# Two-bank PSUM evacuations, LayerNorm's root on another engine and a look-ahead scheduler in a fused attention and feed-forward block

## The chip, the cores and the metric

The kernel runs on one core of a Trainium2 chip. The metric is the time of one execution in microseconds (us), lower is better. A run is one execution; medians and ranges below are over the runs of one kernel. PE is the matmul engine, DVE the vector engine, ACT the scalar engine, POOL the third elementwise engine, and SP the engine that issues most DMA.

"Same" means within 2%.

## The reference

One block with S = 2048 rows, D = 1024, F = 3584 and H = 32 heads of 32:

```python
def _A_ref(x, wqkv, wo):                       # linear attention
    q, k, v = ...                              # x @ wqkv, split into heads
    phi = lambda t: jnp.where(t > 0, t + 1, jnp.exp(t)) + 1e-06
    pq, pk = (phi(q), phi(k))
    kv = jnp.einsum('bhsd,bhse->bhde', pk, v)
    z = jnp.einsum('bhsd->bhd', pk)
    num = jnp.einsum('bhqd,bhde->bhqe', pq, kv)
    den = jnp.einsum('bhqd,bhd->bhq', pq, z)[..., None] + 1e-06
    return (num / den)... @ wo

def _B_ref(x, w_gate, w_up, w_down):
    return _gelu(x @ w_gate) * (x @ w_up) @ w_down

mod = (_silu(c) @ w_mod).reshape(c.shape[0], 6, 1, -1)   # sa, ca, ga, sb, cb, gb
h = _layernorm(x) * (1 + ca) + sa
x = x + ga * _A_ref(h, A_wqkv, A_wo)
h = _layernorm(x) * (1 + cb) + sb
x = x + gb * _B_ref(h, B_w_gate, B_w_up, B_w_down)
```

## The kernel before

The program has eight phases, named here by what PE does: start (modulation, first LayerNorm, the first V rows), K/V/Q projections, merge (the last Q products, the KV matrix, the second modulation set), projection (the denominators and the output projection, then LayerNorm 2), gate/up for half the rows, down, gate/up and down for the other half. The K/V/Q and merge phases use a scheme of seven products where plain blocking needs eight; its elementwise additions run on ACT and DVE, straight from PSUM.

PSUM, the memory that PE writes its results to, is eight banks, cut into small rings. Evacuating a bank means reading a result out of it, so that PE can use the bank again. Each call hands out the next bank of a ring:

```python
class Banks:
    def __call__(self, dt=FP32):
        self.i += 1
        b = psm[:, self.lo + (self.i - 1) % self.n, :]
        return b if dt == FP32 else b.bitcast(dt)
...
QA, QB = Banks(0, 1), Banks(2, 3)
psX = Banks(4, 7)
psC, psB = Banks(0, 3), Banks(4, 7)
```

One bank holds one matmul result of 128x512 float32 (the Trainium skill, "PSUM — Partial Sum Buffer", says the same in its table of terms: one matmul output is at most one bank), so no evacuation in the kernel before has more than 512 columns. In the projection phase, sixteen tiles of 128 rows need two banks each, and two denominators are computed ahead of each tile:

```python
def den_start(b, g):
    psd = psX()
    te.matmul(psd, lhsT=Dbd[:, g, :], rhs=pqT[b][:, g, :], start=True, stop=True)
    lnd = lnd_ring()
    ac.activation(out=lnd, in_=psd, func=AF.Ln, bias=eps6, scale=1.0)      # L876
    rden = rden_ring()
    ac.activation(out=rden, in_=lnd, func=AF.Exp, scale=-1.0)
    return lambda: tt_op(pqT[b][:, g, :], pqT[b][:, g, :], rden, ALU.mult)

def wo_tile(tt, banks):
    ...
    for half in range(NHD):
        cs = slice(half * NW, (half + 1) * NW)
        psw = banks()
        for g in range(KD):
            te.matmul(psw, ...)                                            # L1029
        tt_op(xt[:, cs], psw, xt[:, cs], ALU.add)                          # L480
    gp.dma_start(out=x2_scr[b][tl * P:(tl + 1) * P, :], in_=xt)
    return xt

# projection phase
for tt in range(NTT):
    for _ in range(min(2, len(den_todo))):
        den_start(*den_todo.pop(0))()
    xt = wo_tile(tt, psX if tt < 4 else psC)
    ...
    if tt < 2 * TT:
        ln2_xhat(tt, xt, *ln2_stats(xt, act_rstd))   # LayerNorm 2: two bn_stats, bn_aggr, root, scale
```

`tt_op` is one line for every two-operand DVE operation. In traces it is L480 before the change and L495 after it; experiments that add lines move it to L488 and so on.

The code records operations, and a list scheduler (`Plan`) orders them before they are issued. PE keeps the recorded order. Every other engine is reordered by priority, in forward and backward sweeps over a cost model of the operations, and the order of the best modelled sweep is used.

## Time and profile before

| | before |
|---|---|
| median of the first 3 runs | 772.71 us (772.5 to 773.33) |
| profiled span | 770.3 us |
| PE busy | 752.5 us, 98% |
| DVE busy | 555.1 us, 72% |

The page's table of busy time in the kernel before has one entry for each engine (share of the span, number of instructions); the other line is the summary of the chain of work that ended last, by engine.

```profile
PE 752.5 (98%) x3672; PEld 345.1 (45%) x3697; DVE 555.1 (72%) x1104; ACT 378.1 (49%) x664; POOL 74.4 (10%) x159
PE 82%; DVE 6%; ACT 4%; DMA 4%; issue 1%; POOL 1%; SPq 1%; DVEq 0%; POOLq 0%; ACTq 0%
```

PE is the bound, and all that the other engines do matters only where PE waits for them. The chain is 82% PE and has 10% of DVE and ACT in it, so there are such places. The windows view of the kernel before finds them. Its columns are start:end and length of the stretch, then the busy time of PE, PEld, DVE, ACT and POOL with instruction counts, then the granted clock, the DMA share and GB/s.

```profile
core 0: us, PE busy (x) PEld busy (x) DVE busy (x) ACT busy (x) POOL busy (x), PEclk, DMA share, GB/s
31.60:98.00 66.40, 65.22 (x354) 31.35 (x362) 52.44 (x128) 41.95 (x70) 17.76 (x34) 1.00 0.46 144
170.00:198.00 28.00, 27.64 (x154) 12.01 (x154) 26.90 (x60) 26.51 (x50) 0.00 (x0) 1.00 0.11 35
198.00:225.00 27.00, 24.54 (x110) 10.64 (x110) 25.93 (x59) 19.14 (x41) 6.48 (x12) 1.00 0.60 188
225.00:256.00 31.00, 31.00 (x145) 14.06 (x144) 24.52 (x48) 22.19 (x38) 5.93 (x11) 1.00 0.91 266
```

From 198 to 225 us PE is idle for 27.00 - 24.54 = 2.46 us, while DVE is busy for 25.93 of 27.00 us. The view of waits on PE, for 30 to 440 us of the kernel before, names what ended each idle time (engine, line, what it waited for: total us, times, longest).

```profile
PE psum L874 <- ACT mem L876: 2.2, 2, 1.2
PE psum L1123 <- ACT mem L721: 0.7, 2, 0.5
PE psum L863 <- DVE mem L480: 0.6, 1, 0.6
PE psum L897 <- ACT mem L517: 0.5, 1, 0.5
PE psum L1029 <- DVE mem L480: 0.2, 1, 0.2
```

L874 is the denominator matmul; it waits for the logarithm on ACT (L876) to free its bank. L1123 is in gate/up, L863 in the K/V phase, L897 in the merge. The timeline of PE in the kernel before shows the two long waits (start, duration, operation, in brackets the idle time before it and its releaser):

```profile
205.90 3.66 PE L1029 MATMUL psum<-mem 128*128 128x512 f16 x16
210.51 0.38 PE L874 MATMUL psum<-mem 128*128 128x512 bf16 x1 [0.96 <-ACT mem L876]
212.13 0.38 PE L874 MATMUL psum<-mem 128*128 128x512 bf16 x1 [1.24 <-ACT mem L876]
```

Why is ACT late? Its own timeline in the kernel before answers:

```profile
208.69 0.29 ACT L570 ACTIVATE mem<-mem 128x1 f32<-128x1 f32 x1 [3.58 <-DVE mem L559]
209.77 0.69 ACT L876 ACTIVATE mem<-psum,mem 128x512 f32<-128x512 f32 x1
```

ACT was not busy. Its next instruction in the queue was LayerNorm 2's root (L570), which waited 3.58 us for DVE to aggregate statistics (L559), and the logarithm that PE needed stood behind it. ACT issues its queue in order, as the Trainium skill, "TensorE: Matmul & The Clock Gate", section "Architectural detail: the array is 16× 32×32, not 1× 128×128", says of ACT and DVE; the 3.58 us agree. The groups of the kernel before by form, 168 to 230 us, show what fills DVE (operation, count, busy us, mean ns, idle before):

```profile
L480 DVE TENSOR_TENSOR mem<-psum,mem 128x512 bf16<-128x512 f32 x16 | 11.0, 685 | 0.1
L480 DVE TENSOR_TENSOR mem<-mem 128x512 bf16<-128x512 bf16 x24 | 9.2, 410 | 0.0
L888 DVE SCALAR_TENSOR_TENSOR mem<-psum,mem 128x512 f16<-128x512 f32 x16 | 10.4, 684 | 0.1
```

By these durations a projection tile that also has LayerNorm costs DVE about 2 x 0.69 (additions) + 2 x 0.69 (statistics) + 0.21 + 0.54 + 2 x 0.41 (denominators) = 4.3 us, and PE 18 matmuls of 0.215 us = 3.9 us.

### The profile page before, as it was taken

What the parts mean: (1) busy time and instruction counts of PE and PEld (TensorE: products, weight loads), DVE (VectorE), ACT (ScalarE), POOL (GpSimd) and SP (SyncE); (2) the same over time, 40 slices, a digit from 0 to 9 for tenths busy, and PEclk for the clock granted to TensorE, in tenths of its full rate; (3) what the DMA queues carried; (4) which work ended last, traced back from release to release, by engine and by line L of the source; (5) the groups of instructions that cost most, each with busy time, mean ns of one, the idle gap of its engine ahead of it and who ended that gap; (6) DMA issues with size and microseconds to landing.
All of it is one profiled execution on the core that took longest, in us unless ns stands there. A gap on an engine that the chain in (4) does not pass through costs nothing.

```text
span 770.3 us, 10215 instructions
## 1 busy us (share of the span) xinstructions
PE 752.5 (98%) x3672; PEld 345.1 (45%) x3697; DVE 555.1 (72%) x1104; ACT 378.1 (49%) x664; POOL 74.4 (10%) x159
## 2 busy tenths in 40 slices
PE   6999999999999999999999999999999999999998
PEld 2454445444344444444444444444444444444444
DVE  7878785489997878799887553686777777646254
ACT  3665666569778577775454203215445444430000
POOL 1431300000121122211010000010000000000000
PEclk9999999999999999999999999999999999999999
DMA  9847120780289666766757558852341323355441
GB/s 303 304 131 239 50 69 0 267 321 14 97 243 259 208 209 211 236 196 200 214 181 261 175 195 239 234 156 79 85 110 55 109 72 93 130 184 206 167 153 49
DMA packets 132259, 129.12 MB, mean 168 GB/s; under 512 B 32752, under 2 KB 111216, under 8 KB 131184
## 3 DMA queue, kind: packets, MB, share of 16 engines
q1 hardware_dynamic: 123680, 105.40, 44.2%
q0 software_dynamic: 6176, 20.98, 7.4%
q10 hardware_dynamic: 2352, 2.10, 0.8%
q8 instruction: 29, 0.48, 0.3%
q14 instruction: 22, 0.18, 0.1%
HBM read 98.04 MB, written 23.07 MB: 157 GB/s over the span
## 4 chain that ended last, share of the span: by engine, by line
PE 82%; DVE 6%; ACT 4%; DMA 4%; issue 1%; POOL 1%; SPq 1%; DVEq 0%; POOLq 0%; ACTq 0%
PE psum L1123 41%; PE psum L1228 22%; PE psum L852 5%; PE psum L1029 5%; PE psum L818 4%; PE psum L790 3%; DVE mem L480 3%; DMA mem<-in_A_wqkv_dram 3%; DVE mem L557 1%; DMA mem<-in_B_w_down_dram 1%; ACT mem L709 1%; PE psum L863 1%; ACT mem L721 1%; ACT mem L711 1%; DVE mem L888 1%
## 5 line engine op out<-in xcount | busy, mean ns | idle before, releaser
L1123 PE MATMUL psum<-mem 128*128 128x512 f16 x1568 | 339.1, 379 | 0.7 <-ACT mem L721 0.7
L480 DVE TENSOR_TENSOR mem<-psum,mem 128x512 f16<-128x512 f32 (+4 forms) x296 | 197.9, 680 | 106.8 <-ACT mem L721 39.5
L480 DVE TENSOR_TENSOR mem<-mem 128x1024 f16<-128x1024 bf16 (+9 forms) x415 | 213.8, 539 | 36.5 <-DMA mem<-in_B_w_down_dram 5.4
L1123 PEld LDWEIGHTS <-mem 128*128 128x128 f16 (+1 forms) x1568 | 153.5, 98 | 186.0 <-issue 1.3
L721 ACT ACTIVATE mem<-psum 128x512 f32<-128x512 f32 x226 | 132.2, 594 | 161.9 <-PE psum L1123 81.6
L1228 PE MATMUL psum<-mem 128*128 128x512 f16 (+2 forms) x789 | 169.1, 375 | 0.5
L1228 PEld LDWEIGHTS <-mem 128*128 128x128 f16 x798 | 78.1, 98 | 91.4
L1136 ACT ACTIVATE mem<-mem 128x512 f16<-128x512 f16 x84 | 52.8, 629 | 78.8 <-DVE mem L480 78.7
L852 PE MATMUL psum<-mem 128*128 128x512 bf16 x244 | 57.4, 379 | 1.0 <-DMA mem<-in_A_wqkv_dram 0.2
L1029 PE MATMUL psum<-mem 128*128 128x512 f16 x256 | 57.8, 379 | 0.2 <-DVE mem L480 0.2
L818 PE MATMUL psum<-mem 128*128 128x512 f16 x224 | 51.2, 379 | 0.0
L1029 PEld LDWEIGHTS <-mem 128*128 128x128 bf16 x256 | 24.9, 98 | 32.6 <-DVE mem L480 3.0
L790 PE MATMUL psum<-mem 128*128 128x512 f16 (+1 forms) x168 | 38.4, 379 | 0.1
L852 PEld LDWEIGHTS <-mem 128*128 128x128 f16 x256 | 24.8, 98 | 30.3 <-issue 0.7
L709 ACT ACTIVATE mem<-psum 128x512 f16<-128x512 f32 x40 | 23.6, 593 | 21.4 <-PE psum L852 21.3
L818 PEld LDWEIGHTS <-mem 128*128 128x128 f16 (+1 forms) x224 | 21.4, 98 | 26.6 <-issue 2.1
L557 DVE BATCH_NORM_STATS2 mem<-mem 128x6 f32<-128x512 bf16 x48 | 31.2, 681 | 1.6 <-DMA mem<-in_A_x_dram 1.2
L1008 ACT ACTIVATE mem<-mem 128x512 f16<-128x512 f16 x28 | 20.3, 799 | 18.7 <-DMA mem<-xhs 18.7
L714 DVE TENSOR_SCALAR mem<-mem 128x512 f16<-128x512 f16 x56 | 16.1, 289 | 18.3 <-ACT mem L709 17.9
L790 PEld LDWEIGHTS <-mem 128*128 128x128 f16 x168 | 16.2, 98 | 18.6 <-issue 0.3
L1251 DVE TENSOR_TENSOR mem<-psum,mem 128x512 f16<-128x512 f32 x16 | 11.0, 690 | 17.8 <-PE psum L1228 17.8
L711 ACT ACTIVATE mem<-psum 128x512 f16<-128x512 f32 x40 | 23.7, 595 | 0.0
(115 smaller groups left out, 426.8 us busy)
## 6 DMA issues: line engine op xcount, KB each, us to landing
mem<-in_B_w_gate_dram SPq DMA_DIRECT2D x28, 512.0 KB, 4.1
mem<-in_B_w_up_dram SPq DMA_DIRECT2D x28, 512.0 KB, 5.8
mem<-ts SPq DMA_DIRECT2D x8, 1792.0 KB, 7.0
mem<-in_w_mod_dram SPq DMA_DIRECT2D x24, 512.0 KB, 6.1
mem<-in_B_w_down_dram SPq DMA_DIRECT2D x6, 1792.0 KB, 8.4
mem<-in_A_x_dram SPq DMA_DIRECT2D x32, 256.0 KB, 3.9
mem<-in_B_w_down_dram SPq DMA_DIRECT2D x14, 512.0 KB, 6.3
ts<-mem POOLq DMA_DIRECT2D x14, 512.0 KB, 3.6
```

The costliest lines, as they stand in the source:

```text
L480: ve.tensor_tensor(out=out, in0=a, in1=b, op=op)
L557: ve.bn_stats(out=stats[:, cb, :], in_=xt[:, cb * BW:(cb + 1) * BW])
L709: ac.activation(out=e, in_=t, func=AF.Exp)
L711: ac.activation(out=r, in_=t, func=AF.Relu)
L721: ac.activation(out=t, in_=ps, func=AF.Copy)
L790: te.matmul(ps, lhsT=A[:, k, i * P:(i + 1) * P], rhs=B[:, k, :], start=(start and k == 0), stop=(k == KH - 1), skip_group_check=True)
L818: te.matmul(o, lhsT=W[:, k, (j0 + i) * P:(j0 + i + 1) * P], rhs=h_form(a, k), start=(start and k == 0), stop=(k == KH - 1), skip_group_che ...
L852: te.matmul(ps, lhsT=hr1[b][:, k, tl * P:(tl + 1) * P], rhs=Wk[:, k, n * NW:(n + 1) * NW], start=(k == 0), stop=(k == KD - 1))
L1029: te.matmul(psw, lhsT=pqT[b][:, g, tl * P:(tl + 1) * P], rhs=Wp[:, g, cs], start=(g == 0), stop=(g == KD - 1))
L1123: te.matmul(ps, lhsT=a[:, u, k, :], rhs=b[:, k, :], start=(start and k == 0), stop=(k == KH - 1), skip_group_check=True)
L1136: ac.activation(out=t, in_=src, func=AF.Gelu_apprx_tanh)
L1228: te.matmul(ps, lhsT=a[:, i, q * P:(q + 1) * P], rhs=b[:, i, :], start=(start and i == 0), stop=(i == NPR - 1), skip_group_check=True)
```

## The change

The intent is fewer and larger evacuations. Two neighbouring banks become one tile of 128x1024, and one instruction reads both. The diff, cut to its core:

```diff
+        def pair(self):
+            self.i += self.i % 2
+            self.i += 2
+            lo = self.lo + (self.i - 2) % self.n
+            return psm[:, lo:lo + 2, :]
...
-    qf_ring = Ring(176, [TG], FP32, 6)
+    qf_ring = Ring(176, [2, TG], FP32, 3)
...                                          # LayerNorm 1 of the later blocks
-            rstd = pool_rstd(mv)
+            rstd = act_rstd(mv)
...                                          # V and Q products: copies, additions, phi on pairs
-            for i in range(2):
-                ps = QB()
-                mm(ps, i, "a12", "b21", True)
-                comb(ps, st["p1"][i], i, 0, 0)
+            comb(products(QB.pair(), "a12", "b21", True), st["p1"], 0, 0)
...                                          # Q, block (0, 0)
-                ve.scalar_tensor_tensor(out=dst(i, row, col), in0=..., scalar=0.0, in1=...,
-                                               op0=ALU.max, op1=ALU.add)
+                ve.tensor_scalar_max(out=t, in0=t, scalar1=0.0)      # then a plain addition in phi
...
-    def den_start(b, g):
-        psd = psX()
-        te.matmul(psd, lhsT=Dbd[:, g, :], rhs=pqT[b][:, g, :], start=True, stop=True)
+    def den_pair(b, g):
+        psd = psX.pair()
+        for i in range(2):
+            te.matmul(psd[:, i, :], lhsT=Dbd[:, g + i, :], rhs=pqT[b][:, g + i, :], start=True, stop=True)
...                                          # merge: the KV matrix at one stage, its transposes at the next
-                kv_matrix(1)
-                kv_matrix(0)
+                kv_diagonal()
+            if i == 5:
+                kv_transposes()
...
-            cs = slice(half * NW, (half + 1) * NW)
-            psw = banks()
...
-            tt_op(xt[:, cs], psw, xt[:, cs], ALU.add)
+        tt_op(xt, psw.rearrange("p h n -> p (h n)"), xt, ALU.add)
...
-            for _ in range(min(2, len(den_todo))):
-                den_start(*den_todo.pop(0))()
-            xt = wo_tile(tt, psX if tt < 4 else psC)
+            if den_todo:
+                den_pair(*den_todo.pop(0))
+            xt = wo_tile(tt, psX if tt == 0 else psC)
...                                          # the scheduler, five more sweeps with look-ahead
+                    if look and e != "SP":
+                        soon = [o for o in avail[e] if st < o.ready < st + op.cost and o.due < min(op.due, st + op.cost)]
+                        ...                  # hold the engine for a more urgent operation
-        for _ in range(self.ROUNDS):
-            forward()
+        for i in range(2 * self.ROUNDS):
+            forward(i >= self.ROUNDS)
```

The paired Wp scaling in the merge, the order of one modulation step there, the place of one K product among the Q products of each later block, and the places of some buffers also change.

## The prediction

> What bounds it now. The page's busy table has PE at 752.5 us of a 770.3 us span (98%), clock 1.00 in all slices. All its idle time is 17.8 us, which is a ceiling. The windows view places it: 7.6 us before 15.7 us (first loads and LayerNorm), 0.65 us from 15.7 to 31.6, 1.2 us from 31.6 to 98, 0.3 us to 156, 0.6 us to 170, 0.4 us from 170 to 198, 2.5 us from 198 to 225, nothing to 265, about 1.2 us in the whole rest until 760, and 3.6 us at the end. The built program keeps the same matmuls on PE, with a few neighbours exchanged. The change can win only what PE waits in the phases that it edits (31.6 to 225 us): about 5 us, 0.65%.
>
> What it changes. (1) Two-bank evacuations: pairs of 128x512 operations on DVE and ACT become one of 128x1024. From the groups by form, DVE from PSUM takes 685 ns for 512 columns and 550 ns for 387, so 1.08 ns per column: estimated 1.24 us for 1024 against 1.37 us, 0.13 us saved. All-16-bit DVE additions take 418 ns for 512 and 676 ns for 1024, 0.16 us saved. ACT takes 594 ns for 512; the Trainium skill, "ScalarE: Activation LUTs", section "What ACT_TABLE_LOAD costs", gives 186 ns + 0.833 ns per column for immediates, which agrees (613): estimated 1.04 us, 0.15 us saved. (2) The fused max-and-add of Q (692 ns, twice) becomes a max and a plain addition on 1024, about 0.45 us saved, four times. (3) LayerNorm 1 takes its power on ACT (0.29 + 0.20 us) in place of two POOL instructions (about 1.5 us). (4) The output projection leaves the denominators' PSUM banks after its first tile. (5) The scheduler may hold an engine for a more urgent operation.
>
> What lies on the critical path. From 170 to 225 us DVE is 96% busy (52.8 of 55 us) and the chain of waits runs through DVE and ACT, yet PE is idle only 2.9 us: 2.2 us of it is the denominator matmul waiting for the ACT logarithm to free its bank (two waits, about 211 us), 0.2 us a projection bank waiting for DVE. DVE loses about 69 instructions, some 6 us in that window; the projection's share falls to about 4.0 us of DVE per tile, against 3.84 us of PE. I expect (1) and (4) together to remove about 2.3 us of these, and (3) with the shorter DVE queue about 0.7 us (the 0.6 us wait at 85.6 us and small ones). Against that, a pair is freed later than its first half was: refilled after 1.73 us of other matmuls it leaves ACT or DVE some 0.5 us of slack; I allow 0.3 us of new stalls. The feed-forward part should not move.
>
> Sum: 772.7 - 2.3 - 0.7 + 0.3 = 770.0 us, 80% range 767.8 to 772.6. Faster by over 2% 0.01, within 2% 0.97, slower by over 2% 0.02.
>
> Right if: PE busy stays 752 to 753 us; the two denominator waits near 211 us are gone; DVE's busy total falls by 6 to 12 us, ACT's by about 5; POOL's falls. Wrong if: a PSUM hand-over in the Q/V products or merge stalls PE (waits of PE on ACT copies or DVE additions over 2 us in total); the first K weights land much later than 31.5 us because LayerNorm's writes start earlier; or the new scheduling order reaches the feed-forward part.

## The result

| | before | after |
|---|---|---|
| median | 772.87 us (772.08 to 773.68, 14 runs) | 766.64 us (765.78 to 770.34, 11 runs) |
| ratio of the times | | 0.9927 (0.9916 to 0.9939) |
| profiled span | 770.3 us | 766.2 us; a second trace 764.7 us |

A ratio here and below is of the two kernels' fast runs of the same rounds, with a 95% interval; it is not the ratio of the medians quoted, and can differ from it a little. The change saves 6.2 us or 0.8%. That is "same" at the 2% mark, but it is 1.2 us below the predicted range, and more than twice the gain predicted.

The page of the kernel after, first trace, busy times and the summary of the chain:

```profile
PE 751.1 (98%) x3668; PEld 345.8 (45%) x3697; DVE 547.4 (71%) x1015; ACT 375.3 (49%) x611; POOL 61.8 (8%) x132
PE 93%; DMA 4%; DVE 1%; SPq 1%; issue 0%; ACT 0%; DVEq 0%; ACTq 0%
```

The chain is 93% PE now, and DVE and ACT have almost left it. PE's busy time is no guide here: it fell by 1.4 us only, while the time fell by 6. I read the place of the gain from the start times of matmuls instead. Each row is the time from the first matmul of a phase to the first of the next, from the traces; the two traces of the kernel after are the same program.

```
                    start  K/V/Q   merge  projection  gate/up 1  rest
before              29.45  124.78  37.68  63.78       170.23     same
after, first        30.15  123.80  37.41  61.28       169.21     same
after, second       29.94  123.80  37.41  60.01       169.21     same
second - before     +0.49  -0.98   -0.27  -3.77       -1.02      0.0   sum -5.55 (spans: -5.6)
```

Two denominator matmuls (2 x 0.215 = 0.43 us) moved from the projection to the merge. Free of that, the projection lost 3.34 us of stalls and the merge 0.70 us.

The windows of the kernel after, second trace, same stretches and columns as before (the later stretches now begin some microsecond further into the work):

```profile
31.60:98.00 66.40, 65.92 (x361) 31.84 (x366) 56.19 (x132) 45.12 (x81) 8.99 (x17) 1.00 0.46 145
170.00:198.00 28.00, 27.28 (x150) 12.11 (x152) 24.79 (x35) 25.67 (x27) 0.00 (x0) 1.00 0.12 46
198.00:225.00 27.00, 26.89 (x124) 12.22 (x125) 26.04 (x44) 19.64 (x30) 7.02 (x13) 1.00 0.61 178
225.00:256.00 31.00, 30.95 (x144) 14.10 (x144) 23.73 (x34) 18.16 (x27) 5.42 (x10) 1.00 1.09 304
```

From 198 to 225 us PE has 0.11 us of idle time left. DVE is just as busy as it was by its records (26.04 us), with 44 instructions in place of 59. The waits on PE, 30 to 440 us, in the second trace of the kernel after:

```profile
PE psum L886 <- DVE mem L887: 0.3, 1, 0.3
PE psum L846 <- issue: 0.2, 1, 0.2
```

All five lines shown for the kernel before are gone. The first line here is in the merge (L886 is a Wp matmul); the kernel before has 0.2 us at that product, on a line that the excerpt above leaves out. The timeline of PE at the same place, second trace of the kernel after:

```profile
208.41 0.59 PE L873 MATMUL psum<-mem 128*128 128x512 bf16 x2
208.84 3.62 PE L1026 MATMUL psum<-mem 128*128 128x512 f16 x16
212.29 0.59 PE L873 MATMUL psum<-mem 128*128 128x512 bf16 x2
```

No brackets: two denominator matmuls, sixteen of the projection, two denominators, without a gap. The groups of the kernel after, second trace, 168 to 230 us, answer the question what a pair costs:

```profile
L495 DVE TENSOR_TENSOR mem<-psum,mem 128x1024 bf16<-128x1024 f32 x9 | 11.0, 1218 | 0.0
L495 DVE TENSOR_TENSOR mem<-mem 128x1024 bf16<-128x1024 bf16 x14 | 9.3, 668 | 0.0
L887 DVE SCALAR_TENSOR_TENSOR mem<-psum,mem 128x1024 f16<-128x1024 f32 x8 | 9.7, 1218 | 0.9 <-PE psum L886 0.9
```

By its record, a pair from PSUM takes 1218 ns against 2 x 685 = 1370 ns, and from SBUF, the other on-chip memory (`mem` in the views), 668 ns against 2 x 410 = 820 ns: 0.15 us less each, as predicted (1.24 us and 676 ns). ACT's plain copies from PSUM take 1018 ns against 2 x 594, near the 1039 ns that 186 ns + 0.833 ns per column of the page quoted in the prediction give.

What the pair saves the engine is less. Back to back, the next DVE operation starts 84 ns before the record of the one before it ends. From start to start, in the traces of before and after, an addition of 512 columns from PSUM takes 601 ns and one of 16-bit data 335 ns; the pairs take 1134 and 599 ns (medians of those that follow each other without a gap). So a pair saves about 70 ns in either case, half of what the records show. The Trainium skill, "Perfetto Trace Analysis", section "Optimizing Scalar/DVE Operations", gives about 60 ns of overhead for a DVE operation on SBUF and about 125 ns on PSUM, and adds that the profiled latency is about twice this. This agrees that the record exaggerates (0.15 us by the records, 0.07 us by start times), and for SBUF roughly in size; for PSUM the saving is near half the figure.

By start times, a projection tile costs DVE 2 x 0.60 + 2 x 0.60 + 0.12 + 0.45 + 2 x 0.335 = 3.6 us before and 1.13 + 1.21 + 0.12 + 0.45 + 0.60 = 3.5 us after, against PE's 3.9 us. DVE is the faster one in both. Its lateness is brought along from the merge, and it has a deadline, which the next paragraphs find.

### Which matmul waits

A wait line names a source line, not the tile. Counting the projection's matmuls in the traces gives the place of every stall there (length by start times):

```
before            1.12 and 1.40 us   the two denominators just ahead of tile 4
                  0.37 us            tile 4, sixth matmul of its first half
after, first      1.28 us            tile 14, first matmul
after, second     none
```

Tile 4 is the first tile of the second block of 512 rows. Its eight products take the rows divided by their denominators, g = 0 to 7, and the last of these went into the queues just ahead of tile 3, only 3.9 us earlier. Each has to pass a PE matmul, two ACT operations and one DVE multiplication. So this is the deadline: when PE reaches tile 4, DVE and ACT must have caught up, though they come late out of the merge, where DVE is busy for 26.90 of 28 us. After tile 4 the kernel before stalls no more until the end of the phase, which agrees with a DVE that needs 3.6 us per tile.

The change helps here in two ways: its pairs shorten DVE's and ACT's work ahead of tile 4 (35 DVE instructions against 60 from 170 to 198 us), and it puts five pairs of denominators into the merge where there were eight single ones, so that each denominator is one tile earlier. The experiments take these apart as far as they could.

### Where a wait of PE hides

The view of waits shows 2.2 + 0.2 us of PE waiting in the projection phase before the change; the phase has 3.34 us more of stalls than in the second trace after it. The difference is a property of the records. Matmuls of 512 columns start every 0.215 us, and each record lasts 379 ns, with an end that is modelled. So the first 0.16 us of every stall are covered by the record of the matmul before it, and shorter stalls don't show at all. By start times, the two waits of 0.96 and 1.24 us are 1.12 and 1.40 us, the one of 0.21 us is 0.37 us, and three gaps of 0.12 to 0.15 us appear in no view. (A lone pitch of twice 0.215 us at a full clock is left out of these counts: some matmul records are missing from the traces, as 3672 of PE against 3697 weight loads suggest.) The Trainium skill, "Perfetto Trace Analysis", section "Identifying the Most-Contended Engine", warns that matmul busy time is a poor measure because pipelined matmuls look smaller in the trace. Here their records look longer than their pitch, and the consequence is the same: start times, not busy times, show what PE lost.

### The state of the first trace

The first trace after the change is 1.5 us longer than the second: 1.27 us in the projection and 0.21 us in the start. Two lines of its waits on PE, 20 to 440 us, are in these phases:

```profile
PE psum L1026 <- DVE mem L495: 1.1, 1, 1.1
PE psum L566 <- DMA mem<-in_w_mod_dram: 0.6, 1, 0.6
```

The second, a load of the start, is no mark of the slower trace: it is 1.1 us in the second trace. The first, at tile 14, belongs to a new kind of wait. DVE in the first trace after, 225 to 262 us, has this line:

```profile
DVE mem L1008 <- DMA mem<-xhs: 3.6, 1, 3.6
```

DVE scales and shifts the transposed rows for the feed-forward part (L1008), and their transposed load had not landed. DVE's queue is in order, so a projection addition behind it could not free its banks. No trace of the kernel before's program has this wait. It fits a DVE that arrives at this operation earlier than before, ahead of its data.

### The profile page after: what moved, and what is told of

Read it like the earlier page. It is cut to its first block, busy times and chain, and to the rows that moved or that the text cites. A ratio compares the mean times of both kernels' runs of the same rounds, so it can differ in the third digit from the quotient of the medians.

```text
span 766.2 us, 10016 instructions
## 1 busy us (share of the span) xinstructions
PE 751.1 (98%) x3668; PEld 345.8 (45%) x3697; DVE 547.4 (71%) x1015; ACT 375.3 (49%) x611; POOL 61.8 (8%) x132
## 4 chain that ended last, share of the span: by engine, by line
PE 93%; DMA 4%; DVE 1%; SPq 1%; issue 0%; ACT 0%; DVEq 0%; ACTq 0%
PE psum L1122 44%; PE psum L1227 22%; PE psum L846 7%; PE psum L809 6%; PE psum L1026 6%; PE psum L781 5%; DMA mem<-in_w_mod_dram 1%; DMA mem<-xhs 1%; DMA mem<-in_A_wqkv_dram 1%; PE psum L861 1%; DVE mem L495 1%; PE psum L873 1%; PE psum L512 1%; PE psum L622 0%; SPq L540 0%
## 5 line engine op out<-in xcount | busy, mean ns | idle before, releaser
L495 DVE TENSOR_TENSOR mem<-psum,mem 128x512 f16<-128x512 f32 (+3 forms) x259 | 193.4, 756 | 112.6 <-PE psum L1227 36.0
L495 DVE TENSOR_TENSOR mem<-mem 128x512 f16<-128x512 f16 (+8 forms) x391 | 212.7, 569 | 32.6 <-DMA mem<-in_B_w_up_dram 6.2
L728 ACT ACTIVATE mem<-psum 128x512 f32<-128x512 f32 (+1 forms) x198 | 122.3, 624 | 160.7 <-PE psum L1122 86.6
L852 ACT ACTIVATE mem<-psum 128x512 f16<-128x512 f32 x32 | 19.1, 596 | 19.4 <-PE psum L846 19.1
L723 DVE TENSOR_SCALAR mem<-mem 128x512 f16<-128x512 f16 (+1 forms) x48 | 16.0, 334 | 10.9 <-ACT mem L852 8.5
L1029 POOL DMA_DIRECT2D x2s<-mem x16 | 8.6, 540 | 139.9 <-DVE mem L495 139.9
```

The source lines that it names most:

```text
L495: ve.tensor_tensor(out=out, in0=a, in1=b, op=op)
L728: ac.activation(out=t, in_=ps, func=AF.Copy)
L852: ac.activation(out=e, in_=ps, func=AF.Exp)
```

## Experiments

The theory: PE's stalls in the projection phase are DVE's backlog, passed on through in-order queues, and the pairs remove it; the rest are separate small stalls that different parts of the change remove. The rivals: the banks (a denominator no longer shares a ring with projection tiles), the new look-ahead, LayerNorm 1's root, and chance.

"Phase" lengths below are from start times of matmuls in each run's trace, as above.

### The scheduler: after_again, after_nolook, before_look

The kernel after unchanged, then without look-ahead, and the kernel before with the new scheduler.

```diff
# after_nolook
-            forward(i >= self.ROUNDS)
+            forward(False)
# before_look: sweep() and order() of the kernel after in the kernel before
```

> The changed kernel once more, unedited, for a second trace. In the first trace the start phase was 0.7 us longer than before and PE waited 1.1 us in the projection phase behind DVE. Theory A (those two delays are DMA landings that vary from run to run): the median stays near 766.6 us and this trace shows at least one of the two gone or of another size. Rival (they belong to the schedule): both are there again within 0.2 us.

> The changed kernel with the look-ahead rule of the scheduler off in all ten sweeps; everything else as after. Theory A (look-ahead removed the two stalls of 1.0 us in the first gate/up phase, where ACT was inside a long LayerNorm operation when a PSUM copy was due): about 1.0 us slower than after (767.6), with those stalls back at the first gate/up phase. Rival (the shorter queues of DVE and ACT did it): within 0.4 us of after and no stall in gate/up.

> The kernel before with only the scheduler of the change (ten sweeps, look-ahead in the last five). Theory A: the two stalls in the first gate/up phase (1.0 us) go, the 3.3 us of stalls in the projection phase stay: 771.8 us. Rival C (the new scheduling order is behind most of the gain): 769 us or less.

Measured: after_again 766.63 us (766.47 to 767.86), ratio 0.9924 (0.9912 to 0.9936); after_nolook 767.68 us (766.67 to 768.83), 0.9938 (0.9925 to 0.9950); before_look 773.13 us (772.17 to 774.15), 1.0003 (0.9991 to 1.0015). after_nolook is the kernel after instruction for instruction, and before_look is the kernel before (their traces show the same order on every engine): the look-ahead sweeps never produced a better modelled order, so an order without them was used. The look-ahead does nothing in either kernel. These runs are replicates, and they tell that medians of 5 or 6 runs of one program differ by up to 1 us.

### Banks or pairs: before_banks, after_halves, pairwo_h2act

Three edits share the question. before_banks makes only the change of banks. after_halves keeps everything of the kernel after, banks, tiles and recorded order, but splits each two-bank operation into two of 512 columns again.

```diff
# before_banks
-            xt = wo_tile(tt, psX if tt < 4 else psC)
+            xt = wo_tile(tt, psX if tt == 0 else psC)
# after_halves, one of nine such places
-        tt_op(xt, psw.rearrange("p h n -> p (h n)"), xt, ALU.add)
+        for half in range(NHD):
+            cs = slice(half * NW, (half + 1) * NW)
+            tt_op(xt[:, cs], psw[:, half, :], xt[:, cs], ALU.add)
```

> The kernel before with one edit: the output projection leaves the denominators' PSUM banks after its first tile, as in the change. My prediction's step (the bank sharing causes the two denominator stalls near 211 us): about 2.5 us faster, 770.4. Rival, after the split run (VectorE needs 4.3 us per projection tile against 3.84 us of matmuls, so the stall only moves to another bank): within 0.7 us of before, with 2.5 to 3.3 us of PE stalls still in the projection phase, now on the projection's banks.

> The changed kernel with every two-bank evacuation issued as two one-bank instructions again (V and Q combinations, copies, denominators, Wp, projection additions); banks, scheduler, LayerNorm and the order of the phases stay as after. Theory A (pairing is what cured the DVE queue from 198 to 225 us, and so the denominator stalls): 1.5 to 3 us slower than after, with PE stalls in the merge and projection phases. Rival B (the banks and the scheduler did it, pairing is a side matter): within 0.7 us of after, though DVE is about 8 us busier.

before_banks: 772.33 us (772.15 to 773.01), ratio 0.9998 (0.9983 to 1.0013). The denominator waits are gone, and its waits on PE, 30 to 440 us, show where they went:

```profile
PE psum L1029 <- DVE mem L480: 2.2, 2, 1.4
```

The same 2.2 us stand at the projection now. By count they are the fifth and the sixth matmul of tile 4 (1.58 and 0.99 us by start times). A wait for a bank would stand at the first matmul of a half, so these wait for their operands, the rows that DVE has not yet divided. The banks alone are worth next to nothing (3.1 us of stalls by start times in the phase against 3.3): they decide which matmul waits for the late engines, not how late those are. (All four of its executions also had the lowered clock that is described below.)

after_halves: 771.44 us (770.02 to 772.82), ratio 0.9983 (0.9969 to 0.9996), 4.8 us more than after_again. Its trace is 4.5 us longer than the second of the kernel after: 3.0 us in the projection (63.03 us, 60.01 with pairs), the price of splitting the pairs, and 1.9 us in gate/up, where nothing was split; the rest is 0.5 us the other way. Three of its six executions also had the lowered clock that is described below. The waits on PE of after_halves, 30 to 440 us, show:

```profile
PE psum L1039 <- DVE mem L495: 2.3, 1, 2.3
PE psum L1137 <- ACT mem L728: 1.3, 2, 0.8
PE psum L883 <- ACT mem L887: 0.6, 1, 0.6
```

The backlog is back. L1039 is the third matmul of tile 4, waiting for its divided rows (2.42 us by start times), although after_halves has the earlier denominators and the banks of the kernel after. The timelines of DVE and of PE in after_halves show the two meet:

```profile
210.85 2.05 DVE L495 TENSOR_TENSOR mem<-mem 128x512 bf16<-128x512 bf16 x6
211.28 2.07 PE L1039 MATMUL psum<-mem 128*128 128x512 f16 x6 [2.25 <-DVE mem L495]
```

Six multiplications by the denominators, and six matmuls, the third to the eighth of tile 4. By their times, each of the six matmuls starts about 0.06 us after one of the multiplications ends, so PE goes on at DVE's pitch of 0.335 us in place of its own 0.215. The kernel before does the same at the sixth to the eighth matmul of tile 4 (0.12 us lost at each of the last two). This is the deadline at work, one row group after another. So the banks and the earlier denominators without pairs do not meet it. The second line of the waits is in gate/up, which no part of the edit touches; more on that below.

The opposite direction is before_pairwo: only the projection and the denominators of the kernel before are paired, with the rings, banks, earlier denominators and order of the modulation step that belong to it; V, Q, the Wp scaling, LayerNorm 1 and the KV matrix stay as before. A first draft without the reordered modulation step gave non-finite values, because a pair overwrote the bank of that step.

```diff
# before_pairwo, core
-    def den_start(b, g):
-        psd = psX()
+    def den_pair(b, g):
+        psd = psX.pair()
...
+        psw = banks.pair()
...
-            tt_op(xt[:, cs], psw, xt[:, cs], ALU.add)
+        tt_op(xt, psw.rearrange("p h n -> p (h n)"), xt, ALU.add)
```

> The kernel before with only the denominators and the projection additions paired (with the banks, the small reordering of the second modulation set and the buffers that pairing needs); the V and Q products, K, Wp, LayerNorm 1 and the transposes stay unpaired. VectorE needs about 4.0 us per projection tile in place of 4.3. Theory (its time per tile in the projection phase is what stalls): the stalls of that phase fall from 3.3 us to under 1 us, 769.5 to 771 us. Rival (the backlog comes from the merge phase before it, where V, Q and Wp are still unpaired): over 2 us of stalls stay and the gain is under 1.2 us.

Measured: 774.37 us (771.94 to 778.97), ratio 1.0029 (1.0002 to 1.0056), no faster. Yet in its trace PE is busy for 26.98 of the 27.00 us from 198 to 225 us, as the theory wants. The time went elsewhere, as its waits on PE, 30 to 440 us, show, and those on DVE in 190 to 270 us after them:

```profile
PE psum L1038 <- DVE mem L488: 4.5, 2, 4.2
PE psum L860 <- ACT mem L719: 1.6, 1, 1.6
```

```profile
DVE mem L1020 <- DMA mem<-xhs: 7.0, 1, 7.0
```

DVE stood 7.0 us for the transposed load, with that operation at the head of its queue, and PE 4.2 us behind it, at the first matmul of tile 14, which waits for a bank. This is the wait of the kernel after's first trace, larger. So pairwo_h2act takes the operation that waits off DVE: ACT applies the scale and shift of all transposed rows.

```diff
# pairwo_h2act: before_pairwo, and
-        if h == 0 or kd % 2 or g > 0:
+        if True:
```

> The run with only the denominators and the projection paired, with the same move of the modulation to ACT. Theory (pairing of the projection phase alone cures the stalls near 211 us, and its 774.4 us came from the new wait behind the transposed load, 4.4 us in its trace): the projection phase has under 0.7 us of stalls, and the whole is 769.5 to 771 us. Rival (unpaired V, Q and Wp make a backlog that must stall somewhere): over 2 us of stalls from the merge to the gate phase beyond before's 0.9 us in the merge, 772 us or more.

Measured: 770.85 us (769.88 to 771.79), ratio 0.9974 (0.9960 to 0.9989). The projection phase is 60.19 us long, as in the kernel after, with 0.19 us of stalls. Pairing the projection and the denominators alone, with the banks and the earlier denominators that go with it, cures that phase. Pairs without the earlier denominators were not tried; after_halves shows that the pairs are needed, not that they suffice. The K/V/Q phase became 2.7 us longer (127.52 us), with stalls of 1.72 and 1.11 us where the kernel before has one of 0.81 us (a third, of 0.55 us near 33.8 us, also stands in before_third, so it is no mark of the edit); its recorded operations are the kernel before's, but the scheduler ordered them anew. That this delay of PE gave DVE time to catch up is no likely rival: DVE is busy for only 21.9 of the 40 us from 120 to 160 us in the kernel before, so it had time to catch up before the merge without that delay.

### The size of DVE's load: before_halfstats, after_pad

If the backlog is the cause, taking work from DVE in the kernel before should help as pairs do, and adding work to the kernel after should undo the gain. before_halfstats computes LayerNorm 2's statistics from half the row, which is wrong (the output stayed within the tolerance). after_pad adds a needless addition of 512 columns, 0.41 us, to each of eight tiles; max(x, x) leaves the values alone.

```diff
# before_halfstats
-        mv = ln_stats(x2)
+        mv = ln_stats(x2, 1)                  # one bn_stats of 512 columns in place of two
# after_pad
         tt_op(xt, psw.rearrange("p h n -> p (h n)"), xt, ALU.add)
+        if tt < 2 * TT:
+            tt_op(xt[:, 0:NW], xt[:, 0:NW], xt[:, 0:NW], ALU.max)
```

> The kernel before with a wrong result on purpose: the second LayerNorm takes its statistics from 512 of 1024 columns, one 0.68 us VectorE instruction less in each of the first eight projection tiles (4.3 to 3.6 us per tile). No pairing, no banks changed. Theory (VectorE's time per tile sets the stall of the projection phase): about 3 us faster than before, 770 us, with less than 0.7 us of stalls left in that phase. Rival (the number of instructions, or the banks): within 1 us of before.

> The changed kernel with one added VectorE operation of about 0.41 us (maximum of a half row with itself, result unchanged) in each of the first eight projection tiles: 4.0 to 4.4 us per tile, as slow as before. Theory (VectorE's time per tile): the projection phase grows by 2.5 to 4 us, 769 to 770.6 us. Rival: within 1 us of after.

before_halfstats: 770.37 us (769.91 to 771.15), ratio 0.9972 (0.9957 to 0.9987). The projection shortened from 63.78 to 61.54 us, with 0.54 us left at tile 4, and gate/up lengthened by 2.0 us, with stalls of 1.14 and 1.86 us. after_pad: 773.63 us (772.86 to 774.15), ratio 1.001 (0.9993 to 1.0026), so 8 x 0.41 = 3.3 us of DVE work cost 7.0 us. All four of its executions had the lowered clock described below, which is part of that. Its projection is 66.85 us, 6.85 more than in the kernel after. The timeline of PE in after_pad:

```profile
210.92 0.61 PE L1026 MATMUL psum<-mem 128*128 128x512 f16 x2 [0.49 <-DVE mem L495]
215.04 3.46 PE L1026 MATMUL psum<-mem 128*128 128x512 f16 x10 [3.51 <-DVE mem L495]
218.29 1.06 PE L873 MATMUL psum<-mem 128*128 128x512 bf16 x2
```

Both point the way the theory says; both miss in size. By start times, after_pad stalls for 0.65 and 3.67 us at the fifth and the seventh matmul of tile 4, and for 0.81 us at the end of the phase: 5.1 of the 6.85 us. Only four of the padded tiles come before tile 4, so the stall there is longer than the 4 x 0.33 us (by start times) that were added ahead of it: the in-order queue has been arranged anew by the scheduler, and how that makes 4.3 us of it is not settled. The remaining 1.7 us took two more runs to understand (below): after the long stall, matmuls start every 0.427 us in place of 0.215 for 3.4 us (seven of them, and one at each end in part). The last two lines show it: two matmuls of L873 take 1.06 us there, and 0.59 us in the trace of the kernel after.

### The clock after a stall: before_third, before_fourth

The trace of before_look, the same program as before, also has such a stretch at a pitch of 0.427 us after its two denominator waits, and the first trace of the kernel before has none. The two further runs are the kernel before, unchanged, to see which is the rule.

> The kernel before, unchanged, for a further trace. Found after the other runs: in the trace of the same program that was taken in the scheduler run, eight matmuls after the two denominator stalls (1.12 and 1.40 us) start every 0.427 us in place of 0.215 us, at a granted clock of 0.72 in 212 to 218 us, which costs 1.7 us; in the first trace of the kernel before, with the same stalls, none does. If the lowered clock is a matter of chance (a window of observation that does not start with the program, as the Trainium skill, TensorE: Matmul and The Clock Gate, Part 1, says), the projection phase of this trace is either near 63.8 us or near 65 to 65.5 us, and no other place of the trace shows a pitch of 0.427 us. The rival, that the length of the stall alone decides, expects the same pitch as in one of the two traces only if the stall has its length too; a stall of the same length with the other outcome contradicts it.

> As before_third: the kernel before, unchanged, once more. Chance expects either outcome again at the same two stalls; no pitch of 0.427 us elsewhere between 31 us and the end.

Measured: 773.79 us and 772.18 us, one run each. Both have the two stalls at the same length (1.12 and 1.40 us by start times). The windows view of before_third, then of before_fourth:

```profile
212.00:218.00 6.00, 5.50 (x17) 2.00 (x18) 4.84 (x12) 4.28 (x9) 1.02 (x2) 0.72 0.64 210
```

```profile
212.00:218.00 6.00, 5.11 (x22) 2.07 (x23) 5.76 (x15) 5.08 (x10) 1.08 (x2) 1.00 0.60 174
```

The granted clock (third from the end) is 0.72 in one and 1.00 in the other, and PE completes 17 against 22 matmuls. The projection phase is 64.91 us in the first and 63.78 in the second. So after equal stalls the clock dropped in one execution and not in the other. The length of the stall alone doesn't decide it. The Trainium skill, "TensorE: Matmul & The Clock Gate", section "What's actually happening", says that the clock is halved by a monitor of PE's activity with a free-running window of 3413 ns, and its next section gives 426.7 ns as the pitch of 512 columns at the half rate and 215.7 ns at the full one. This agrees: pitches of 0.427 and 0.215 us, and a mean of 0.72 over 6 us, which is 6 x 0.28 / 0.5 = 3.4 us at half rate.

The traces can also test whether the window's position is what differs. They keep the times at which the granted clock changed (no view prints them). In each of the 20 traces, all these changes lie whole multiples of 3.413 us apart, to within 0.002 us. So the windows can be laid back over the stalls, and PE's idle time in each can be summed from start times. In before_third the fullest window holds 2.12 us of idle time and in before_look 2.52 us, and the clock drops where that window ends; in before_fourth the same stalls are cut by a window's edge, the fullest window holds 1.91 us, and the clock stays. Over all traces, from the first K matmul to the end, the six windows at whose end the clock dropped hold 2.12 to 3.12 us, and no other holds more than 2.13 us (the first trace of the kernel before). The half rate then lasts one window, or two in before_pairwo. So what decided here was how much idle time fell into one window, with a limit near 2.1 of 3.41 us, an estimate from these traces.

The mean clock of each execution is recorded with its time, so this can be counted. A stretch of 3.4 us at half rate lowers the mean of a 770 us execution to 0.998. Of 48 executions of the kernel before's program whose clock is on record, 25 are at 0.998 or lower, and of 22 of the kernel after's none is. In the 41 of those 48 that ran beside other kernels, the median span of the 21 lowered ones is 771.1 us and of the 19 at 1.00 it is 770.5 us. So the clock costs the kernel before about 0.6 us in half of its executions, some 0.3 us on average: a part of the gain, but a small one. In kernels with longer stalls it costs more. before_pairwo's two executions at 1.00 have spans of 770.7 us in the median, and the two lowered ones 775.5 us; in its trace the long stall and the drop come together, and 770.7 us is near the kernel before's time. The trace of before_pairwo is one of the slow pair.

### LayerNorm 1's root: after_poolrstd, before_poolcost

```diff
# after_poolrstd, in the LayerNorm of later blocks
-            rstd = act_rstd(mv)
+            rstd = pool_rstd(mv)
# before_poolcost: only the scheduler's cost model, in the kernel before
-            op.cost = 200 + n / 0.5
+            op.cost = 600 + n / 0.5
```

> The changed kernel with the reciprocal root of LayerNorm 1 back on POOL. My prediction's step: worth about 0.7 us with the queue, so 767.1 to 767.6, with a stall of 0.6 us or more back in the K/V phase. Rival (the K/V stall of before was an accident of the recorded order, as it was also absent in the run with other banks): within 0.4 us of after, no stall above 0.3 us there.

> The kernel before with a scheduler that counts 600 ns in place of 200 ns as the fixed cost of a POOL operation (the trace has 0.24 to 0.87 us). Theory (the 0.8 us stall in the K/V phase and the two in the first gate/up phase, 1.0 us, come from ACT operations that the scheduler places too early behind POOL results, with PSUM copies queued behind them): both go, 1 to 1.8 us faster than before, 771.1 to 771.9. Rival (those stalls come from DVE and ACT load): they stay, within 0.4 us of before.

after_poolrstd: 768.90 us (767.89 to 769.47), ratio 0.9949 (0.9937 to 0.9962), 2.3 us more than after_again, which ran in other rounds (1.9 us by the two ratios). The K/V/Q phase is 1.62 us longer, with stalls of 0.72, 0.55 and 0.37 us. The 0.55 us, near 33.8 us, come and go among traces of one program (0.15, 0.28 and 0.55 us in three of the kernel before's), so the root accounts for about 1.1 us of the 1.62. The waits on PE of after_poolrstd, 30 to 440 us, have one of these, and the gate/up phase, 1.3 us longer, has the other line:

```profile
PE psum L1122 <- ACT mem L728: 0.8, 2, 0.5
PE psum L861 <- DVE mem L495: 0.6, 1, 0.6
```

before_poolcost: 772.67 us (771.31 to 774.93), ratio 1.0003 (0.9981 to 1.0026). With a model that knows POOL's small operations to be slower, the K/V/Q phase of the kernel before fell to 123.65 us, the kernel after's length. So it was the order around a late POOL result that made the stall there, and either ACT's root or a truer cost removes it (this run doesn't have the moved K product, which therefore isn't needed for it). The median does not show it, because two of the four runs had the lowered clock. The other two have spans of 769.5 and 769.6 us, about 1 us less than the 770.5 us of the kernel before at full clock; two runs are few.

### The KV matrix: after_kvtogether

```diff
                 kv_diagonal()
-            if i == 5:
-                kv_transposes()
+                kv_transposes()
```

> The changed kernel with the eight transposes of the KV matrix back in the same merge stage as the products that feed them. Theory: the two PE stalls there (0.63 + 0.27 us before) return, 0.7 to 1.0 us slower than after. Rival (the shorter VectorE queue hides them): within 0.4 us.

Measured: 767.49 us (766.72 to 768.04), ratio 0.9935 (0.9921 to 0.9949). The merge is 38.29 us, 0.88 us longer than in the kernel after, and the kernel before's stall is back in its waits on PE, 30 to 440 us:

```profile
PE psum L899 <- ACT mem L532: 0.5, 1, 0.5
```

The median difference of 0.9 us is within what replicates differ by, but the trace shows the stalls: PE's transposes came before the matrix was ready, and one more stage of Q products between them covers that.

### The start and the transposed load: after_start, after_h2act, after_h2late, after_h2act_pool

Four tries for a better version.

```diff
# after_start: one more V product ahead of the first step that waits for the modulation weights
-        for n, tl in ((0, 0), (0, 1), (0, 2), (0, 3), (1, 0), (1, 1)):
+        for n, tl in ((0, 0), (0, 1), (0, 2), (0, 3), (1, 0), (1, 1), (1, 2)):
-        sa.columns(modT[:, 0:KD], 0.0, lambda: v_plain(2, 1))
-        v_plain(3, 1)
+        sa.columns(modT[:, 0:KD], 0.0, lambda: v_plain(3, 1))
# after_h2act: scale and shift of transposed rows on ACT
-        if h == 0 or kd % 2 or g > 0:
+        if True:
# after_h2late: the cost model's time of a transposed load
-        plan.transpose = (6000, 1000000)
+        plan.transpose = (9000, 1000000)
# after_h2act_pool: after_h2act, and POOL's cost 600 + n / 0.5
```

> A try at a faster version: the changed kernel with one more V tile multiplied before the last modulation row is needed, since PE waits 0.3 to 1.8 us for that load in every trace of the changed kernel. If that wait is free to be hidden: 0.3 to 1.0 us faster than after. Rival (the loads of the start are one stream at full DMA use, so the wait moves to the first K weights or to the shorter shadow for the LayerNorm shift): within 0.4 us.

> The changed kernel with all modulation of the second LayerNorm's transposed rows on ACT, so that no VectorE operation waits for the transposed load. Theory (VectorE, now ahead of its work, sits 1.5 to 3.9 us at the head of its queue behind that load, with projection additions behind it, and this gives part of the run-to-run spread of 765.8 to 770.3 us): no PE stall above 0.3 us from 225 to 256 us, median 0.3 to 1 us under the changed kernel's, spread smaller. Rival (the spread is all in the start's loads): within 0.3 us, same spread.

> The changed kernel with the scheduler counting 3 us more for the second LayerNorm's transposed load (9000 in place of 6000), which puts one more projection addition ahead of the modulation on VectorE and changes no instruction. Theory of the wait at the head of the queue: PE stalls from 225 to 256 us under 0.4 us, and 0 to 0.7 us faster than the changed kernel. Rival: no change, or new stalls elsewhere by a new recorded order (gate/up phase over 0.5 us).

> The move of the modulation to ACT together with a truer POOL cost in the scheduler (600 ns fixed). If the stalls of the first gate/up phase come from POOL results that the scheduler expects too early, none is above 0.3 us there and the whole is 765.5 to 766.5 us. Rival (they come and go with any new order): a stall above 0.3 us appears there in this trace.

| | median (range), runs | ratio to before | seen in the trace |
|---|---|---|---|
| after_start | 769.19 (767.29 to 773.82), 6 | 0.9961 (0.9939 to 0.9983) | the wait for modulation weights is gone, 0.81 us appear after it; 1.59 us behind the transposed load; gate/up 1.3 us longer |
| after_h2act | 766.94 (766.69 to 767.61), 5 | 0.9926 (0.9914 to 0.9937) | no wait of DVE for the transposed load; projection 60.27 us |
| after_h2late | 768.20 (767.5 to 772.37), 6 | 0.9947 (0.9926 to 0.9968) | a stall of 3.09 us in the projection, then half-rate matmuls; 64.91 us |
| after_h2act_pool | 766.65 (766.21 to 768.17), 4 | 0.9923 (0.9909 to 0.9938) | projection 60.26 us, gate/up 169.21 us |

None beats the kernel after by more than its replicates differ. after_h2act removes the new wait, and its range is narrow (0.9 us), where that of the kernel after's first 11 runs is 4.6 us with two executions above 768.5; that the wait makes those slow executions fits but is not shown, since they were not traced. after_h2late missed its expectation: telling the scheduler that the load is slower put the waiting operation at a place where PE stalled for 3 us. after_start missed too.

## Why the prediction was right or wrong

The predicted time was 770.0 us, and the measured one is 766.64 us, outside the range of 767.8 to 772.6. "Within 2%" was right. The step that failed is the size of what PE loses and the change can win back: the prediction added up waits of the views (2.3 us in the projection, 0.7 us in K/V/Q), gave the merge nothing but new stalls, and said "The feed-forward part should not move". The gain was 6.2 us against 2.7 predicted. By start times, the missing 3.5 us are about 1.0 us in the projection term, 1.0 us in gate/up, which was set at nothing, 1.0 us in the merge, which was set at a loss of up to 0.3, and 0.3 us in term (3); the small rest is the clock and the loads of the start. Its terms:

**"I expect (1) and (4) together to remove about 2.3 us of these": the mechanism was right and the size wrong.** The term measured 3.3 us. It was sized with the idle time that the views of PE show, 2.2 + 0.2 us, and the views hide up to 0.16 us of each stall and all the shorter ones. "All its idle time is 17.8 us, which is a ceiling" is no ceiling for the same reason, though the gain stayed below it. Sharing the term between (1), the pairs, and (4), the banks, was also too generous: before_banks shows that (4) alone is worth next to nothing, after_halves that without pairs 3.0 us of the projection's gain are gone, and pairwo_h2act that the pairs, banks and earlier denominators of this phase together are enough. The earlier denominators were not named in the prediction at all. The kernel before also loses some 0.3 us on average to a lowered clock after these stalls, which the prediction had no term for.

**"The projection's share falls to about 4.0 us of DVE per tile, against 3.84 us of PE": wrong picture.** By start times it is 3.6 us before and 3.5 after; DVE does not set the pace of the tiles, it is late at one deadline, tile 4. The saving of a pair, 0.13 and 0.16 us predicted, is right for the records and about 0.07 us for the engine. What (2), the split of the fused maximum in Q, was worth was not measured apart.

**"The feed-forward part should not move": wrong.** Gate/up for the first half gained 1.02 us between the two traces (169.88 to 170.46 us in four traces of the kernel before's program, 169.21 to 169.27 in three of the kernel after's, so 0.6 to 1.25); no line of it changed. In the kernel before it has two stalls, one of which the timeline of ACT explains:

```profile
336.52 1.24 ACT L993 ACTIVATE mem<-mem 128x1024 f16<-128x1024 bf16 x1 [0.95 <-POOL mem L992]
337.67 1.06 ACT L721 ACTIVATE mem<-psum 128x512 f32<-128x512 f32 x2
```

ACT waited for a POOL result at the head of its queue, and the copy from PSUM that PE needed stood behind. Where such an operation lands in the queue is the scheduler's affair. Over the variants the stalls of this phase range from 0 to 3.0 us, with no line of it edited: 0.28 us in before_banks, 0.35 us in before_poolcost, 1.95 us in after_halves, 3.0 us in before_halfstats, 0 in the kernel after. The prediction had this under "wrong if: the new scheduling order reaches the feed-forward part", but gave it no size. A scheduler's model that takes POOL for too fast fits (after_h2act has 0.35 us of stalls there, after_h2act_pool none; before_poolcost has less than before), but it is not proven for the phase as a whole. This 1.02 us is luck of the order more than a merit of the change.

**"(3) with the shorter DVE queue about 0.7 us": near.** The K/V/Q phase gained 0.98 us, and the root's part is shown by after_poolrstd, which gives about 1.1 us back in that phase.

**The merge was overlooked.** The prediction allowed it only new stalls. Splitting the KV matrix removed its stalls of 0.63 and 0.27 us, as after_kvtogether shows by bringing them back; less the new stalls below, the merge gained 0.70 us.

**"I allow 0.3 us of new stalls": about right.** The merge lost 0.90 us of stalls and became 0.70 us shorter, so some 0.2 us are new; the one that the view shows is at the Wp pairs (L886). Not foreseen was the wait of DVE for the transposed load, up to 3.6 us in the traces of the kernel after, of which PE felt 1.1 us in one trace of three and nothing in the others.

**"(5) The scheduler may hold an engine":** it does not; the built programs are the same with and without.

**The signs.** The two waits near 211 us are gone: right. DVE's busy time fell by 7.7 us (6 to 12 predicted): right. ACT's fell by 2.8 us (about 5 predicted): too high, as ACT took over the root (24 more instructions of 0.25 us). PE busy "stays 752 to 753" came out at 751.1 and 750.0 us: with modelled ends, busy time contains some of the stalls that were removed.

The sum, from the first trace before to the second after: projection -3.34, K/V/Q -0.98, gate/up -1.02, merge -0.70, start +0.49, so -5.55 us, and the spans say -5.6. The medians differ by 6.2 us; the half-rate clock in half of the executions before accounts for about 0.3 of the rest. The start's +0.49 us is the landing of loads, which differs among traces of one program (29.42 to 30.97 us in four of the kernel before's), and needs no explanation by the change.

## What to carry to other kernels

When PE is 98% busy, measure its losses by the start times of matmuls, phase by phase, and count which matmul waits; idle times in the views are a lower bound, and a few stalls that add up to two or three microseconds within 3.4 may also be followed by matmuls at half rate. A wait that is put down to one engine can belong to another whose result stands at the head of an in-order queue, so ask what that engine itself waited for, and what it will wait for once it is faster. Where a scheduler orders the whole program, an edit in one phase moves stalls of about a microsecond in others: compare the built programs first, and count such gains apart from those of the change's own mechanism.

## What the Trainium skill lacked or had wrong

- "Perfetto Trace Analysis", section "Identifying the Most-Contended Engine": it says pipelined matmuls look smaller in the trace. In these traces they look longer than their share: records of 379 ns at a pitch of 215 ns, which hides up to 0.16 us of every stall of PE.
- "TensorE: Matmul & The Clock Gate", section "HAM oscillation — how this bites in real kernels": it states the abstract rule as no idle gaps above about 3.4 us. Taken by itself that is too weak here: two gaps of 1.12 and 1.40 us, 1.6 us apart from start to start, were enough in about half of the executions (25 of 48 at a mean clock of 0.998 or lower), and the half rate then lasted 3.4 us. By the traces, idle time of 2.12 to 3.12 us in total within one window of 3.41 us was followed by half rate in six traces.
- "Perfetto Trace Analysis", section "Optimizing Scalar/DVE Operations": by its figure, about 125 ns of overhead for DVE on PSUM would be saved by joining two operations. By start times 68 ns were (2 x 601 to 1134 ns), and 71 ns on SBUF (2 x 335 to 599 ns), where the page has 60. The section could say by how much records overlap back to back: 84 ns on DVE.
- No page that I read puts a price on a waiting operation at the head of an in-order queue: 3.58 us of ACT behind DVE's statistics before the change, and 7.0 us of DVE behind a transposed load in before_pairwo, of which PE felt 4.2 us.
